# Sparse attention and a gated feed-forward block on one core: all transposes moved to TensorE

## The chip, the cores and the metric

The kernel runs on one core of one Trainium2 chip. Its engines are TensorE (PE; its weight loads are listed as PEld), VectorE (DVE), ScalarE (ACT), GpSimd (POOL) and SyncE (SP, which here only issues DMAs). The metric is the device time of one launch in microseconds (us), as the median of several runs. The profile is of one more execution, whose own time is given beside its span.

## The reference

Inputs are q, k and v of 4 batches, 8 heads, 768 positions and 64 dimensions, in float32, and the three matrices of a gated feed-forward block. Heads 0, 2 and 6 attend causally to everything; the other five see only the first 4 positions (the "sinks") and the last 64.

```python
def _attn_ref(q, k, v, is_retrieval, n_sink, window):
    scores = scale * np.matmul(q, k.transpose(0, 1, 3, 2))
    stream_keep = causal & (is_sink | in_win)
    mask = np.where(retr, full_mask, stream_mask)
    scores = np.where(mask[None, :, :, :], scores, -1000000000.0)
    a = np.exp(scores - np.max(scores, axis=-1, keepdims=True))
    a = a / (np.sum(a, axis=-1, keepdims=True) + 1e-09)
    return np.matmul(a, v)
# x: the heads side by side, 3072 x 512; d_ff = 1536
def _moe_ref(x, w_gate, w_val, w_out):
    g = x @ w_gate
    silu = g * (1.0 / (1.0 + np.exp(-g)))
    return silu * (x @ w_val) @ w_out
```

## The kernel before

**Tiles.** Positions are cut into 24 tiles of 128, six per batch. Two neighbouring tiles are a pair: 12 pairs in the order of the list `QP`, which takes batches 0 and 1 in turn and then 2 and 3. Four tiles make one of six groups `g` for the feed-forward part, whose moving operand is then 512 columns wide.

**Attention.** For a pair `n`, q, k and v (called `x` in the names of the loads) are loaded as float32 into one of 11 `raw` buffers (`load q5`), and cast to float16 (`cq5`, `ck5` into `hq`; `cx5.m.j` into `vt`). Queries and keys then have to be turned, so that the 64 dimensions (of two heads) lie on the partitions. There are two ways of doing that. For pairs 0 to 4 (`n < XPE`) PE turns eight 128x128 blocks with an identity matrix into one bank of PSUM (`trq`, `trk`, L473), and two copies on ACT or DVE take them to `qT` or `kT` (`evq5.m`, `evk5.m`, L206 and L208). For pairs 5 to 11 two transposing DMAs, issued on SP, do it from SBUF to SBUF (`dq5.m`, `dk5.m`, L463). The two ways leave positions in different orders, so the exponentials of the later pairs permute their output. Loads differ with them: pair 0 and pairs 5 to 11 are read in runs of 512 bytes by one DMA of 512 KB (L354), pairs 1 to 4 in runs of 2 KB by two DMAs of 256 KB (L349).

For a tile `t`, scores are made in up to four units (`sc5.0`, L567) in PSUM, ACT takes the exponential (`ex5.0`, L579), DVE or POOL multiplies with a 0/1 mask (`mask5.0`, L587; the first four tiles have the mask added by PE instead), PE multiplies with the values (`val5.1`, `val5.0`, L597) and DVE normalizes (`nm5`, L604 and L605) into `xb`. The columns of sink keys and values are copied to where later tiles find them (`sk`, `sv`).

**Outputs of attention.** `xb` has positions on the partitions; the feed-forward part needs features there. For tiles 0 to 7 (`t < XBAR`) PE turns four blocks (`xtr5`, L621) and ACT or DVE copies them into `xt` (`xe5`). For tiles 8 to 23 one transposing DMA on SP writes `xt` (`xdma8`, L615).

**Feed-forward.** For each group and each of 12 slices `j` of d_ff: four matmuls with gate weights (`gate2.3`, L759), a tanh on ACT (L765), a product on DVE (`stt1`, L769), four matmuls with value weights (`vals2.3`, L759 too), a product on DVE into `h_sb` (`stt2`, L775). The output product of groups 0 to 4 is done in seven products of half-size blocks in place of eight (`out2.p1` to `p7`, L839), with sums of `h_sb` blocks (`hs`, L826, POOL or DVE) ahead and sums out of PSUM (`oe`, L855, DVE) behind. Group 5 does it plainly (`out5`, L793). Results are stored by `st` on SP or ACT.

**What sets the order.** Every step is a task with dependencies, which are turned into semaphore waits. No scheduler runs: the string `ORDER` lists all tasks, in the order in which they are recorded, and each engine executes its own tasks in that order. `WAYS` says for each task which of the allowed engines does it (for example DVE or POOL for a mask), `SLOTS` which buffer of a ring, or which bank of PSUM, it takes. Numbers from 3700 up in `ORDER` are groups of warm-up matmuls (L321) for PE. Loads on SP stand in the same order, and a load waits there until its `raw` buffer is free, with all later DMAs of SP behind it.

Of the kernel before, what the change touches and what calls it, by code (L numbers as in the profile page):

```python
# [13 lines left out]


ORDER = (
    "0306071W091U1V1X000A08xy1c0D0C01050B1d1e040gy01f1gzJ1i1h2021282922232B1j1r1s021p1q1w0F2C2D2E2F1b"
    "2A2L2M2N2O2X2f2g0m1Y1a1Z1t1u1v1k0h252h1l1m2W2c242G2H2I2d2e2l2m2i2j0G271n1o1y1z3C262P2Q2R0z2t3031"
    "2J0y8e8o2n2K102U2o2p3I3J2V8t8j8m8u8v8k8l8n1x2k8f8g8p8q2x382y8h8i118r8s8w8x138y8z9893909495999A33"
    "340n9D9E0E2Z3K3D3L3M3N149B9C9F969G9H972a9192322b2Y2q2r2s2u3R3S3W3X0k1C9c9d9e9h9i9j3U3V3O2z353P36"  # L20
    "39370q1D9f9g9k9l3T3b3i3n3o3f3g0H3H3E3F2v2w0i169I9J9K9N9O9P0o179L9Q9R9M0l1F3Q3Y3Z3c3j3a0I3u40410j"
    "193k3h9m9n9o3l3m3A3B9S9T9U9r9s9t3d3e9X0J3v4344453G3p3q3r0r1G9u9p9v429Y9Z3s3t0x1H2S4647494A4H0p1A"
    "9V9WB74N4O4Q4R0K3z9q9zA10N4c3x4BB4B5B6B8Ak4K4L4V4b4C4D3yAT484M0w0sAQARASAU9a9b9y0t1E0W6K2TAlAmAV"
    "AWAX151M1O1N1PAYAZBEAfAgAhB9BABB4a0u181Q1R1SBCBDAp0v1BBFBGA0AaAbAnAoAc3wBHBIAdAe0L0M0PB20T12A41I"
    "1J1K0S4d4P0O4Z4h4g4Y4e4f5D5L5K0RAzB0B1AqArB31L0YALAM0ZAN4E4F4G4J4I6J1TAuAvAOAPAw9wA2A69xA3A7A55C"
    "5I5JAA4l4m4i4j4kACA8A9ABAD4n4v51524y53AiAj5f5lAEBMAGAFAK4S4z504T4W4UAxAy5g5nAsAtBL4q4r4o4p54BO0c"
    "AHAIAJ4s554t4u4x4wBJBKBQ56575T5U6MBNBP5W5c5XBb5j0X58595A5B707S7T6xBVBW6wBRBS5i5VBXBYBc6z5YBZBaBd"
    "5p5qBT5s605t5u4XBsBtBuCeCbCcCdCfCMCNCOCCBvBwCDCE0V6I5v0Q5F5G5H6v5k5o5M5N5O0UBiBjBk5rCPCQBlBm5E5Z"
    "5a5b5d5wCHCICJCWCXCY5m63696A666768Bh5h73CKCLC7C8C9710eCRCS5P5Q5R6465CACBCTBUC2C36y7Q6P74BnBo5x5y"
    "5z610a72CZCaBp5S625e6H6NBqBrC46B6C6F6D6GCFCGCiBeBfBgBxByBz7O7UC0C1C5C681CUCVCjCl6E6U6V6W6X6Y6R6S"  # L30
    "6T6eDmDjDkDlDnDoDpDqDrDs0b7P7X7WDtDuDv6Z6aCgChCn6b6c6d6fDUDVDWDXDY7576776g7C7D7E7F7G7L0dDwDxCkCm"
    "DSDFDGDHDPDQDRDT7b7c7d6QDADBDCDyDzE0DDDE7H80D5D6D7CsCt6O6n6o6h6i6j6kE1E27V7I7J7M7K7ND8D96l6m7879"
    "7A7BCoCpCrCuCv897Y7Z6p6q8786DKDLDMDZDaDb6L6r6s6t6uDcDdDeDfDgCwCx7e7f7R7j7m7n7o7p7q7rDNDOCyCzD0D4"
    "EhEiEjErEsEcEd88EkElEtCqD1D2D3EuEvEeDhDi7a7g7h7k7iFLFMFNFOFP7x8D8E8A8I8B8C8F8JFJFGFHFIFKFBFCFDDI"
    "DJE5E77s7t8GFEFFEp7u7v7y7w8HEXEYEZ0f838485EmEnEoEqEfEg8NEw8Y8ZE6E88T8U8VEzExEyF0EBE3E9E4EAECEDF6"
    "828K8L8M8OF1F2F3F9EFEG8Q8R8S8W8XEVEHEIEJF7F8FA7l8P7z8a8b8cEaEbESETEUEWEEEOELEM8dGiGMGTGUEKGCENER"
    "G7GVGWGjGkGJGKEPGREQFTFVGXGLGOGPGEGFGNGQG9F4GAGSGGGYGbGZF5GaGcGBGDFSGHFpFqFrFQFRG4G5GdGeFzFUFeFW"
    "FXGIG6G0G8FcFdGfFfFuFvFYFaFbGgGhG1G2G3FsFtFxGlGmFZFwFyFlFiFjFmFnFgFhFkFoGnGoGpGsGtGuGvGwGqGrGxGy"
    "GzH0H2H3H4H5H7H1H6H8H9"
)  # L40
WAYS = (
    "000010000000000000000000000000000000000000000000000000000000221202202202212200200111000111110010"
    "222200001100000000000000220022122022001011000000000000001100212002000011001001000001000001001000"
    "000201021120001000001001000000010010000010000000002221220000000000010000002000100100000020000221"
    "000000000100000002000010010000000000020200000010000000000000110000011000000100100000020001000000"
    "002202200220000000000000000012000100100000000201120000000000000000010002202202010000001001000001"
    "200000000000011002021000000000000000000200000000000000000000000000000000000000000000000000000000"
    "000000000000000000000000000000000000000000001000000000000000000000000000000000000000000000000000"
    "000000000000000000000000000000001000000010000000000000000000000000000000000000000000000000000000"
    "000000000000000000001110100011000000000001000000000000000000000000000000000000000000000000000000"  # L50
    "000000001111000001100000000000100000000000000000000000000000000000000000000000000000000000000111"
    "101100110000000000011000000000000000000000000000000000000000000000000000000000000000010000100000"
    "00000010"
)
SLOTS = (
    "0014237653916A152371476981504A39A2564807049A28352A9168410016041002241601230163620442561014104122"
    "636011642065221025144416322211256461406003404624344620616540610143626540604164236062324342142254"
    "041614064616325426212246140636104325614261306242452460436460636014122636230644521206164434062601"
    "020211341120003102001134000210400214105510131201001011040122021303213020111113411111040020200051"
    "014110101310002114301212131010022102320210013012111032112010000012000102211130011112010111054125"  # L60
    "001050101010110200030111402521014010311140310020120011321112001301101022015010340000101100015042"
    "1331142120102320202014112511225023512531113120100101201"
)
DIGITS = "0123456789ABCDEFGHIJKLMNOPQRSTUVWXYZabcdefghijklmnopqrstuvwxyz"

# [54 lines left out]
def kernel(  # L120
# [13 lines left out]
    nc = tc.nc  # L134
# [36 lines left out]
    P = Plan(RINGS)  # L171
# [38 lines left out]
    def recast(task, dst, src):  # L210
# [24 lines left out]
        out=ident, in_=ident, compare_op=ALU.not_equal, fill=1.0,  # L235
# [97 lines left out]

    XPE = 5
    XOLD = 1

    landed = {}
# [27 lines left out]
    for kd, n in ([(kd, n) for n in range(NP) for kd in "qkx"]  # L367
                  + [(kd, n) for kd in "gvo" for n in range(6)]):
        T_iss[kd, n] = P.add(f"load {kd}{n}", ["SP"], (lambda kd=kd, n=n: load(kd, n)),
                             takes=["raw"])  # L370
# [49 lines left out]
                                 (lambda i=i, x=x: wsum(i, x)),  # L420
                                 deps=[T_w["o", i][0], T_w["o", i + 3][0]] + before))

    XBAR = 8

    LEAD = 4

    hqs = {}
# [29 lines left out]
    def turned(n, kd):  # L457

        b, pi = QP[n]
        return qT[n % QB] if kd == "q" else kT[b % 2][:, 2 * pi:2 * pi + 2]  # L460

    def dmat(n, kd, m):
        nc.sync.dma_start_transpose(  # L463
            out=turned(n, kd)[:, m].rearrange("c k r (j n) -> c (k r j) n", j=2),
            in_=hqs[n, kd][m * 64:(m + 1) * 64].rearrange("p k a x -> p (k a x)"))

    trs = {}

# [100 lines left out]
    def exps(t, u, unit):  # L569
        e = es[t, u] = buf("e", [128, 8, 128], FH, "e")  # L570
        for p, s_, c, kt in unit[0]:
            h = PAIRS[p][s_]
            av_blocks.setdefault((t, h), []).append((e[:, c, :], value(t, h, kt)))
        at = slice(min(c for _, _, c, _ in unit[0]), unit[1])
        to, src = e[:, at], whole_sc.pop((t, u))[:, at]
        if t // 2 >= XPE:
            to = to.rearrange("p c (n j) -> p c n j", j=2)
            src = src.rearrange("p c (j n) -> p c n j", j=2)
        nc.scalar.activation(out=to, in_=src, func=AF.Exp, scale=scale)  # L579

    def mask(task, t, u, m):
# [27 lines left out]
    def xtranspose(t):  # L609
        xb = xbs.pop(t)  # L610
        g, n = GROUP[t]
        if g not in xts:
            xts[g] = buf("xt", [128, 4, 512], FH, "xt")
        if t >= XBAR:
            nc.sync.dma_start_transpose(  # L615
                out=xts[g][:, :, n * 128:(n + 1) * 128],
                in_=xb.rearrange("p a b d -> p (a b d)"))
            return
        tr = buf("gv", [128, 4, 128], FH, "xtr")
        for p in range(4):  # L620
            nc.tensor.transpose(tr[:, p, :], xb[:, p].rearrange("p a d -> p (a d)"), ident)  # L621
# [12 lines left out]
    def tasks_of_pair(n):  # L634
# [40 lines left out]
    def tasks_of_tile(t):  # L675
# [344 lines left out]
```

## Time and profile before

| | |
|---|---|
| median of 3 runs | 246.04 us (245.84 to 246.38) |
| profiled execution, its own time | 246.15 us |
| its span, first to last instruction | 244.4 us |
| granted TensorE clock | 1.00 of full speed |
| HBM read and written | 28.31 MB and 6.29 MB |
| gate and value matmuls, L759, 128x512 | 544, 216 ns from one to the next in a gapless stretch |
| PE transposes, L473 and L621 | 80 and 32, of 128x128 |
| transposing DMAs, L463 and L615 | 28 and 16, 1.2 us each to issue, 2.7 to 3.1 us to land (medians) |
| loads of q and k, L354 / L349 | 16 of 512 KB / 16 of 256 KB |

"Busy" is the time in which an engine had an instruction running; matmuls overlap, so the mean length of one (379 ns for 512 columns) is more than the time that it holds PE. The idle time of a group is what its engine waited just ahead of it, with the engine and line that released it. A released wait is put down to the last event seen.

### The profile page before, as it was taken

What the parts mean: (1) busy time and instruction counts of PE and PEld (TensorE: products, weight loads), DVE (VectorE), ACT (ScalarE), POOL (GpSimd) and SP (SyncE); (2) the same over time, 40 slices, a digit from 0 to 9 for tenths busy, and PEclk for the clock granted to TensorE, in tenths of its full rate; (3) what the DMA queues carried; (4) which work ended last, traced back from release to release, by engine and by line L of the source; (5) the groups of instructions that cost most, each with busy time, mean ns of one, the idle gap of its engine ahead of it and who ended that gap; (6) DMA issues with size and microseconds to landing.
All of it is one profiled execution on the core that took longest, in us unless ns stands there. A gap on an engine that the chain in (4) does not pass through costs nothing.

```text
span 244.4 us, 5604 instructions
## 1 busy us (share of the span) xinstructions
PE 234.5 (96%) x2189; PEld 143.6 (59%) x2189; DVE 186.7 (76%) x324; ACT 148.5 (61%) x235; POOL 129.0 (53%) x140
## 2 busy tenths in 40 slices
PE   7989999998999999799999999999999999999995
PEld 3667855553457678445555457656456764475743
DVE  0577887889999999887987977669769777776800
ACT  3899899887878669487637776563682302330011
POOL 7479999956497552375765446910094110375000
PEclk9999999999999999999999999999999999999999
DMA  6999999999766989999464451519100213100053
GB/s 187 355 348 353 323 352 366 313 362 305 206 131 78 287 165 289 191 268 192 89 130 130 97 120 38 90 36 234 38 4 0 46 21 115 59 0 1 7 203 136
DMA packets 66794, 40.73 MB, mean 167 GB/s; under 512 B 25168, under 2 KB 60240, under 8 KB 66768
## 3 DMA queue, kind: packets, MB, share of 16 engines
q1 hardware_dynamic: 65392, 37.76, 61.5%
q10 hardware_dynamic: 1376, 2.62, 2.9%
q8 instruction: 17, 0.28, 0.5%
q14 instruction: 9, 0.07, 0.1%
HBM read 28.31 MB, written 6.29 MB: 142 GB/s over the span
## 4 chain that ended last, share of the span: by engine, by line
PE 54%; DVE 19%; issue 8%; DMA 6%; POOL 5%; SPq 5%; ACT 2%; DVEq 0%; POOLq 0%
PE banks L759 34%; PE banks L839 10%; PE banks L793 4%; DMA raw<-in_moe_w_val_dram 4%; DVE h_sb L775 4%; PE banks L567 3%; DVE h_sb L826 3%; SPq L349 3%; DVE sil L769 3%; PE banks L597 2%; POOL hs_sb L826 2%; DVE out_sb L855 2%; DVE xb L605 2%; DMA xt<-xb 2%; DVE e L587 2%
## 5 line engine op out<-in xcount | busy, mean ns | idle before, releaser
L759 PE MATMUL banks<-xt,wg_sb 128*128 128x512 f16 (+1 forms) x304 | 70.3, 368 | 1.9 <-DMA xt<-xb 1.4
L759 PE MATMUL banks<-xt,wv_sb 128*128 128x512 f16 (+1 forms) x304 | 70.4, 368 | 0.8 <-DVE sil L769 0.7
L579 ACT ACTIVATE e<-banks 128x1024 f16<-128x1024 f32 (+2 forms) x68 | 58.7, 910 | 20.0 <-PE banks L567 11.7
L765 ACT ACTIVATE sig<-banks 128x512 f32<-128x512 f32 (+1 forms) x76 | 43.0, 577 | 43.5 <-PE banks L759 37.5
L769 DVE SCALAR_TENSOR_TENSOR sil<-sig,banks 128x512 f32<-128x512 f32 (+1 forms) x76 | 49.0, 656 | 14.8 <-ACT sig L765 12.6
L775 DVE SCALAR_TENSOR_TENSOR h_sb<-sil,banks 128x512 f16<-128x512 f32 (+1 forms) x76 | 48.7, 656 | 6.7 <-PE banks L759 4.4
L587 POOL TENSOR_TENSOR e<-e,m 128x640 f16<-128x640 f16 (+1 forms) x22 | 37.8, 1727 | 27.2 <-ACT e L579 24.3
L759 PEld LDWEIGHTS <-wg_sb 128*128 128x128 f16 x304 | 28.5, 98 | 30.7 <-issue 3.1
L759 PEld LDWEIGHTS <-wv_sb 128*128 128x128 f16 x304 | 28.2, 98 | 29.5 <-issue 1.2
L839 PEld LDWEIGHTS <-h_sb 128*128 128x128 f16 x360 | 34.8, 98 | 7.9 <-issue 0.7
L826 POOL TENSOR_TENSOR hs_sb<-h_sb 128x768 f16<-128x768 f16 x7 | 11.5, 1640 | 40.9 <-DVE h_sb L775 29.4
L855 DVE TENSOR_TENSOR out_sb<-banks,out_sb 128x512 f32<-128x512 f32 x35 | 23.6, 685 | 4.7 <-PE banks L839 4.4
L826 POOL TENSOR_TENSOR h_sb<-h_sb 128x768 f16<-128x768 f16 x11 | 18.0, 1639 | 8.2 <-PE banks L839 4.4
L839 PE MATMUL banks<-wo_sb,h_sb 128*128 128x256 f16 x180 | 21.9, 273 | 0.0
L839 PE MATMUL banks<-wt_sb,h_sb 128*128 128x256 f16 x180 | 21.5, 273 | 0.4 <-DVE out_sb L855 0.4
L567 PE MATMUL banks<-qT,kT 64*128 64x128 f16 x472 | 20.6, 218 | 1.1 <-DVE xb L605 1.0
L567 PEld LDWEIGHTS <-kT 64*128 64x128 f16 x472 | 14.6, 94 | 11.0 <-issue 10.2
L597 PEld LDWEIGHTS <-e 128*128 128x128 f16 x472 | 17.1, 97 | 4.3 <-ACT vt L206 0.9
L597 PE MATMUL banks<-vt,e 128*128 128x65 f16 x472 | 18.2, 193 | 1.0 <-POOL vt L208 0.7
L605 DVE TENSOR_TENSOR xb<-banks,rc 128x512 f16<-128x512 f32 x24 | 16.6, 691 | 0.8
L208 POOL CAST vt<-raw 64x512 f16<-64x512 f32 x22 | 14.4, 654 | 4.8 <-DMA raw<-in_v_dram 2.3
L206 ACT COPY out_sb<-banks 128x512 f32<-128x512 f32 (+1 forms) x7 | 4.0, 570 | 19.1 <-PE banks L793 16.0
(60 smaller groups left out, 216.3 us busy)
## 6 DMA issues: line engine op xcount, KB each, us to landing
raw<-in_v_dram SPq DMA_DIRECT2D x12, 512.0 KB, 7.0
raw<-in_q_dram SPq DMA_DIRECT2D x8, 512.0 KB, 4.8
raw<-in_k_dram SPq DMA_DIRECT2D x8, 512.0 KB, 5.1
raw<-in_moe_w_gate_dram SPq DMA_DIRECT2D x6, 512.0 KB, 8.9
raw<-in_moe_w_val_dram SPq DMA_DIRECT2D x6, 512.0 KB, 8.4
raw<-in_moe_w_out_dram SPq DMA_DIRECT2D x6, 512.0 KB, 7.9
out_dram<-out_sb SPq DMA_DIRECT2D x6, 512.0 KB, 4.7
raw<-in_q_dram SPq DMA_DIRECT2D x8, 256.0 KB, 6.4
```

The source lines that it names most:

```text
L567: nc.tensor.matmul(sc[:, c:c + n, :], weights, moving, start=first, stop=last)
L579: nc.scalar.activation(out=to, in_=src, func=AF.Exp, scale=scale)
L587: ENG[task().way].tensor_tensor(out=ev, in0=ev, in1=mm, op=ALU.mult)
L597: nc.tensor.matmul(avs[t][:, odd, n * 66:n * 66 + 65], ee, vv, start=(m == 0), stop=(m == len(bl) - 1))
L605: nc.vector.tensor_tensor(out=xb.rearrange("p n o d -> p o n d"), in0=av[:, :, :, 0:64], in1=rc.to_broadcast([128, 2, 4, 64]), op=ALU.mult)
L759: nc.tensor.matmul(ps, wsb[:, kk, j * 128:(j + 1) * 128], xt[:, kk, c[0]:c[1]], start=(kk == 0), stop=(kk == 3))
L765: nc.scalar.activation(out=sg[g, j, c], in_=gs[g, j, c], func=AF.Tanh, scale=0.5)
L769: nc.vector.scalar_tensor_tensor(out=sl[g, j, c], in0=sg.pop((g, j, c)), scalar=1.0, op0=ALU.add, in1=gs.pop((g, j, c)), op1=ALU.mult)
L775: nc.vector.scalar_tensor_tensor(out=hs[g, j][:, c[0]:c[1]], in0=sl.pop((g, j, c)), scalar=0.5, op0=ALU.mult, in1=vs.pop((g, j, c)), op1=A ...
L826: ENG[T_hs[g, x][part].way].tensor_tensor(out=to, in0=a, in1=b, op=op)
L839: nc.tensor.matmul(rooms[g, p][:, x], left[:, j, 128 * x:128 * x + 128], right[:, j], start=(j == 0), stop=(j == NK - 1))
L855: nc.vector.tensor_tensor(out=cell(*to), in0=rooms[g, p], in1=cell(*other), op=ALU.add)
```

## The change

- `XPE` goes from 5 to 12, so queries and keys of all pairs are turned by PE and copied out of PSUM, and pairs 1 to 11 are loaded in runs of 2 KB. `dmat` and its tasks go.
- `XBAR` goes: the attention outputs of all tiles are turned by PE (`xtr`) and copied by DVE or ACT (`xe`).
- The exponentials no longer permute positions for the later pairs.
- `ORDER`, `WAYS` and `SLOTS` are new throughout. By the lists of each engine's instructions, DVE and ACT between them get 28 more copies into `qT` and `kT` and 16 more into `xt`; nine masks go from DVE to POOL, and five sums `hs` too; four stores go from ACT to SP. The warm-up matmuls are 24 instead of 21.

```diff
-    XPE = 5
+    XPE = 12
     XOLD = 1
...
-    XBAR = 8
-
...
-    def dmat(n, kd, m):
-        nc.sync.dma_start_transpose(
-            out=turned(n, kd)[:, m].rearrange("c k r (j n) -> c (k r j) n", j=2),
-            in_=hqs[n, kd][m * 64:(m + 1) * 64].rearrange("p k a x -> p (k a x)"))
...
         to, src = e[:, at], whole_sc.pop((t, u))[:, at]
-        if t // 2 >= XPE:
-            to = to.rearrange("p c (n j) -> p c n j", j=2)
-            src = src.rearrange("p c (j n) -> p c n j", j=2)
         nc.scalar.activation(out=to, in_=src, func=AF.Exp, scale=scale)
...
-        if t >= XBAR:
-            nc.sync.dma_start_transpose(
-                out=xts[g][:, :, n * 128:(n + 1) * 128],
-                in_=xb.rearrange("p a b d -> p (a b d)"))
-            return
         tr = buf("gv", [128, 4, 128], FH, "xtr")
         for p in range(4):
             nc.tensor.transpose(tr[:, p, :], xb[:, p].rearrange("p a d -> p (a d)"), ident)
...
-            if n >= XPE:
-                T_ev[n, kd] = [P.lands(P.add(
-                    f"d{kd}{n}.{m}", ["SP"], (lambda n=n, kd=kd, m=m: dmat(n, kd, m)),
-                    deps=cs[kd] + old)) for m in range(2)]
-                P.uses(cs[kd][0], "hq", *T_ev[n, kd])
-                continue
             tr = P.add(f"tr{kd}{n}", ["PE"], (lambda n=n, kd=kd: transposes(n, kd)),
                        deps=cs[kd], takes=["gv"], after=[T_warm])
...
-        if t < XBAR:
-            xt = P.add(f"xtr{t}", ["PE"], (lambda t=t: xtranspose(t)),
-                       deps=norms, takes=["gv"] + takes, after=[lead])
-            T_xe[t] = P.add(f"xe{t}", ["DVE", "ACT"], (lambda t=t: xevac(t)), deps=[xt])
-            P.uses(xt, "gv", T_xe[t])
-            P.uses(norms[0], "xb", xt)
-        else:
-            xt = P.add(f"xdma{t}", ["SP"], (lambda t=t: xtranspose(t)), deps=norms,
-                       takes=takes, after=[lead])
-            T_xe[t] = P.lands(xt)
-            P.uses(norms[0], "xb", T_xe[t])
+        xt = P.add(f"xtr{t}", ["PE"], (lambda t=t: xtranspose(t)),
+                   deps=norms, takes=["gv"] + takes, after=[lead])
+        T_xe[t] = P.add(f"xe{t}", ["DVE", "ACT"], (lambda t=t: xevac(t)), deps=[xt])
+        P.uses(xt, "gv", T_xe[t])
+        P.uses(norms[0], "xb", xt)
```

More of the change, by code (lines that the diff above doesn't have):

```diff
@@ L16 @@
 ORDER = (
[L17 to L36, printed above, removed]
@@ L37 @@
-    "G7GVGWGjGkGJGKEPGREQFTFVGXGLGOGPGEGFGNGQG9F4GAGSGGGYGbGZF5GaGcGBGDFSGHFpFqFrFQFRG4G5GdGeFzFUFeFW"
-    "FXGIG6G0G8FcFdGfFfFuFvFYFaFbGgGhG1G2G3FsFtFxGlGmFZFwFyFlFiFjFmFnFgFhFkFoGnGoGpGsGtGuGvGwGqGrGxGy"
-    "GzH0H2H3H4H5H7H1H6H8H9"
+    "000402061U1V071W03xx1c1d1e0920211Xy21f0C01050A22yG28292A231g1h1i1j1r1s1p1q1w081Z1b1axh2B2CzG2E2D"
+    "2F2N2O2L2M2W2c2d2e0B2426252G2H2I0D2X2f1Y1k1l1m1t1u1v2g2i2h2j2l2m1n2J1o1y1z2K272P2Q2R0g0y98999A1x"
+    "2t30312x382y0F3C3I3J3K0h139c9S9T9d9U0m109B9C0n140G2o2p33349e0z9I2S2U2V9D9G9h9a9E9F9H9i9j2n9V9W0E"
@@ new lines @@
+    "2Y2a2Z9X9Y9Z9f9g9b9J9K3D3L2b2k2q2r2s2u3M3N3O3P3U3V329k9l0i169r9m9s9t2z9n9o3R3S353637399N9O119L9M"
+    "9P9Q9R0H3F3H3E3b3l3m3i3j0l1FALAGAMANAH3W3X3f0o179u9v9pAI9q3T3G0q1D3Q3Y3Z3a3g3c0k1CA6ABA7A83kA9AA"
+    "ACAD2T0j3n3o0t19A19wA23h3p3q2v3r3A3B2w3d3e0r1GAJAKA3AOAP3s3t0J3v439x9y0I3u4041420p1AA4A50K3y3x3z"
+    "Ax0U15AEAFATAV4446454748494H4A4BB40wAuAvAwAy9zA00P5J0M4b0u18ASB5B6BEBFBGBdBeBf0s12B7B84L4M4NB9BA"
+    "BBBYBZBgBhBaBC1E1M3w0V4O4P4W4CBbBc4DAUBDAzB0B14j4k4l0RBiBjBk0x1H1Q1R1T1S4E4F4GBHBIBlBm0vB2B31B1K"
@@ new lines @@
+    "1I1J1LAY1N1P0L4a4g4h4i5R0N4d4f4e4cAQAXARAZAW4p4qBTBUBVBOBPBQ4m4z4R4S5S5TApAqAr0bBWBX1OAe0O5I0Y7E"
+    "4n4oBJBKBL0S0e4Q5O5P5Q4I0W6X6YAcAdAfAiAj4r56574J4KAaAbAgAhAkAo4T4U4V4X53AsAt5p5v5w54554u4v4s4t5f"
+    "BMBN4w5g4x4y505c5l5dBRBSBpBrBnBo5B5C595A58AlAm4Y4Z515D5E5F5xBv0T5s5t520a5q5y5z60BqBsBuByC5Bt6465"
+    "0cAnBw616C625G5HC10Z7H66D5D6D7CCCDCECoD8D90Q5L5K5NClCmCnCp7mCRCSCTCgChCi5h6J6KBzC07M7N7O5rCjCk0X"
+    "7D5M5e5i5j5k5mC36VC2C4C6C7CB7I6W6L5U5V5W6G6H6ID0D1D2CvCwCFCGCxCe5X5Y5ZCMCNCyCzCO7lD3D467685u7k6M"
@@ new lines @@
+    "6N6e6f6gCUCV6b6c6d63696A6B6DCPCQCqCrCs5a5n5b5o7q7r7s6O6P6Q6SCbCcCdCf7J7K6E6FCWCXCYBxC8C9CA7L6R6h"
+    "6i6j6k6l6uCtCu6T6UCKCZCaDDDFCHCICJENEOEPCLDCDE6mEDEEEFDtDuDv7t7u7v0f8T6n6o6p6qEIEJ0d8QDADGDBDH7o"
+    "7X7Y7Z7a7g7b7cDwDxEKELEMEGEH6r6s6v6tDIDLDJ8U74757172737P7Q7RDeDfDgDyDzE0EQERDZDaDb7z807G76DhDiES"
+    "ETEUE1E2EVEW6aDMDN7F7d777e7f7S7T7U8RDm6y6z707w7xDcDd6w6x7i7V7W7j7pE3E4E5DODPDj6Z78797AE881DkDlDn"
+    "8W8X8Y7B7CDoDpDqEB7nFBFCFD878H8I8B8CE9DQDR7yE6E7EA8E8MEC8283FLFMFNFEFFDrDs7h848588868ZFOFPFn8D8F"
@@ new lines @@
+    "8G8a8b8c8k8l8f8g8h8d8e8VFGFHFIFaFbFcF6F7F8FiFVFWDKF9FAFXDSEZDUEaDTEbFkFlFJFKFmDYFfFgDVDWFoFhFj8J"
+    "8K8N8LEXEYEdFpFqFrFsFtFQFRFS8p91928w8xFdFe8i8j8tFTEcElEe8S8m8n8o8q8uEfEi8vF1F2EjF3En8z90EwExEhFU"
+    "Es8y9394DXEkEmEgEo898r8A958s8OF49697EpEqErEtEz8PGxHCHDGnFxFzEyH2GyF5GbGzGqEvGoEuF0GpGrGiGjH0H5Gk"
+    "GvH3H1H4H6GsGtGuGwFYFZGlGYGZGaGcGJGKGLFuFvFwFyG0G2G4GdGeGfGmH7H8H9GRGgGhGOGPGTHEGUG1G6G7G5GFHAG3"
+    "GCHBGVGWGXGAGQGSHFHGGMGNG8G9GDGGGHHHGBGEGIHIHJHMHNHKHLHOHRHPHQHSHTHWHXHYHbHUHVHZHaHcHd"
@@ L40 @@
 )
 WAYS = (
[L42 to L51, printed above, removed]
@@ L52 @@
-    "101100110000000000011000000000000000000000000000000000000000000000000000000000000000010000100000"
-    "00000010"
+    "000010000000000000000000000000000000000000000000000000000000222202022222202002220010101010101212"
+    "020000000000000000000000110001212222011011000000100000001000220011011000001001000001001001001000"
+    "000001220111011000001001000000010000010010000000002201120000000000010000000010010010000011000200"
+    "200010010010010000000210100100000000000020102000001100000001001001000010002221101000000100100000"
@@ new lines @@
+    "020000100100000120120000201100000000100000002200001001000000000220112000000001000000010010001101"
+    "201110001001000001000001101001001000001201102020000000001000000000010010000010000000000000000000"
+    "000000000000000000000000000000000000000000000000000000000000000000000000100000000100000000000000"
+    "000000000000000000000000000000000000000000000000000000000000001001000100000000000000000000000000"
+    "000000000000000000000000000000000000000000000000001111110011000000000000000000000000000000000000"
@@ L54 @@
+    "000000000000000000000000000000000000000111110000100000000000100000000000000000000000000000000000"
+    "000000000000000000000000000111110100110000000000000000000000000000000000000000000000000000000000"
+    "00000000000000000000000010000000000010"
 )
 SLOTS = (
-    "0014237653916A152371476981504A39A2564807049A28352A9168410016041002241601230163620442561014104122"
-    "636011642065221025144416322211256461406003404624344620616540610143626540604164236062324342142254"
-    "041614064616325426212246140636104325614261306242452460436460636014122636230644521206164434062601"
@@ L59 @@
[L59 to L62, printed above, removed]
+    "0015246374927435A772A445A6315997824058A38A501609221819001016041002241222230063601254461440016340"
+    "656011214224222121043652064614232261606014354644521622063602461221046162644040343654462621302145"
@@ new lines @@
+    "600160216141211426361623606445601310362216320614025604224614041421402642562542516163424201406465"
+    "604133263222541412634461606200005010410210124411031120024500140040110012330130002110011155022233"
+    "031050200011002221015001401011100100401441250120510120130251113012411115121401501220005100430000"
+    "013110000200100345500000202121500000211114301100125115412010041125124052131203005501111211023311"
+    "1112131134100412210200023310531201144125302011050100012411241100410131043120200002102"
```

## The prediction

> **What bounds the kernel now.** I read the page's busy shares first, then the busy time by stage, then the chain that ended last, and last the groups by shape.
>
> ```profile
> PE 234.5 (96%) x2189; PEld 143.6 (59%) x2189; DVE 186.7 (76%) x324; ACT 148.5 (61%) x235; POOL 129.0 (53%) x140
> ```
>
> Busy time in five stages from the first value matmuls on (columns: stretch, its length, then PE, PEld, DVE, ACT, POOL busy, granted clock, DMA share, GB/s):
>
> ```profile
> 22.65:61.00 38.35, 37.60 (x393) 22.63 (x393) 32.66 (x65) 34.23 (x58) 32.59 (x34) 1.00 1.11 337
> 61.00:100.00 39.00, 38.16 (x402) 26.86 (x399) 37.96 (x64) 28.84 (x42) 21.32 (x19) 1.00 0.89 186
> 100.00:140.00 40.00, 38.25 (x332) 20.49 (x333) 32.89 (x58) 26.65 (x43) 24.72 (x21) 1.00 0.78 161
> 140.00:200.00 60.00, 59.12 (x574) 37.25 (x573) 46.16 (x77) 31.37 (x50) 23.11 (x21) 1.00 0.32 66
> 200.00:244.40 44.40, 41.38 (x247) 23.40 (x244) 25.05 (x39) 9.29 (x16) 11.40 (x7) 1.00 0.19 72
> ```
>
> PE idles 0.75, 0.84, 1.75 and 0.88 us in the four stages up to 200 us, 4.22 us in 177. Nothing else is so full, except DVE between 61 and 100 us (37.96 of 39.00). DMA is full only until about 61 us. Pieces of the chain that ended last (start, length, what):
>
> ```profile
> 28.34 0.45 PE banks L473 x8
> ...
> 45.64 0.22 PE banks L621 x4
> ...
> 95.85 0.50 SPq L615
> 96.40 4.70 DMA xt<-xb
> 101.24 5.34 PE banks L759 x24
> ...
> 200.24 13.81 PE banks L759 x64
> ...
> 230.99 10.40 PE banks L793 x60
> ```
>
> Three things are in it. From 200 us to the end PE runs without a gap (64 matmuls of 512 columns in 13.81 us are 0.216 us each), so anything that delays PE before 200 us delays the end. The one place where a transposing DMA holds PE is at 101.24. And it prices the operations that the change multiplies: eight L473 transposes hold PE for 0.45 us, 0.056 us each, and four L621 transposes for 0.22 us, 0.055 each. The 0.22 us "mean of one" in the groups is latency, which overlaps.
>
> [...]
>
> **PE, added.** Pairs 5 to 11 get PE transposes for q and k: 7 x 2 x 8 = 112 at 0.056 us = 6.3 us. Tiles 8 to 23 get four each: 64 at 0.055 = 3.5 us. Together +9.8 us of PE time, in the new order all between about 60 and 200 us, where PE has 4.22 us free in all. Nothing PE does is taken away there: scores, values, gates and products are the same in number and shape. Lower end: if all 4.22 us of idle were filled, +5.6. Upper end: were each group to hold PE for its whole latency (0.62 us for eight L473, 0.40 for four L621, from the timeline of PE), 14 x 0.62 + 16 x 0.40 = 15.1. I take 9.8, since the groups in the chain, which stand between other matmuls, hold PE for just 0.45 and 0.22.
>
> [...]
>
> **PE, removed.** The wait at 101.24 for the first transposing DMA of tile 8 (idle 1.4 us, "DMA xt<-xb" in the groups): -1.4. It is the only PE wait put down to a DMA; q and k transposes by DMA have none. Ends: 0, if the PSUM copy that replaces it is as late, and -1.5.
>
> **What is late next.** Each group now needs a copy out of PSUM before its reader can run, on ACT or DVE, in their order. I walked the new order of PE and looked for readers that stand within 2.2 us of PE work behind their transposes. After 60 us there are six: trk7 before sc14.1 (1.3 us: out1.p5), trk11 before sc22.0 (1.7), trq5 before sc10.1 (1.8), xtr11 before gate2.11 (1.3), xtr17 before gate4.3 (1.7), xtr23 before gate5.8 (2.2). A pair of ACT copies takes 1.06 us (2 x 0.59, overlapped), so each is covered unless one or more other instructions stand ahead of the copy: for k of pair 7 it is xe10, 0.59. Bounds: 0 to 6 x 0.59 = 3.5 us. I take one copy's length, 0.6, since most have cover and PE's queue behind the waiting matmul is then stopped (here all of group 2's gates). The other waits of PE in the old order (4.22 - 1.4 = 2.8 us up to 200) belong to that order; the new one has its own, by the same kinds of edges, and I carry them over at equal size, 0 net, with -2.8 as the end if they go.
>
> **The other engines.** ACT gets 14 kT, 5 qT and 9 xt copies (0.588, 0.590, 0.586 us): +16.5, and gives up casts and sink copies, net +7.7. DVE gets 9 qT and 7 xt copies (0.683, 0.419): +9.1, plus value casts, but nine masks leave it, net +4.1. POOL takes those masks (five at 2.122, four at 1.397 us: 16.2) and five more sums at 1.64, net about +26. I price all of this at 0: ACT is 52 to 74% busy from 61 to 200 us, POOL 39 to 62%. DVE is the one to fear: up to the last value matmuls of tile 11 (93.9 us now) its work grows by 1.8 us, but PE's grows by 2.2 by then. If that cover went, the price would be those 1.8 us. POOL's masks are slow (2.1 us against 0.784 on DVE) and in front of the value matmuls; a mask that is late costs at most the 1.3 us difference, which is inside the 3.5.
>
> **Loads and queues.** Fourteen loads of 512 KB in 512-byte runs become 28 of 256 KB in 2 KB runs, an extra 14 issues on SP at 0.60 us (L349), 8.4 us. From the same queue go 44 transposing issues at about 1.2 us, 53 us. All of it lies after the first 30 us, where SP is not what PE waits for: price 0. Stores move from ACT to SP, and four waits there end later, 0. The early loads are the same in bytes and shape; v0 goes behind g1 and k2 back two places. By the same landing times gate0.2 would take v0's place, so the head moves by no more than one load, within 0.6 us either way. Exponentials lose a permuted write: the rows of old and new kinds of tile are both 1.02 us, 0. Three more warm-up matmuls stand in the head, where PE waits for loads, 0.
>
> **Sum.** 246.15 (the profiled execution: 244.4 of span and 1.8 around it) + 9.8 - 1.4 + 0.6 = 255.15. The median of the runs is 0.11 lower than that execution, so 255.0.
>
> **Rivals.** *The new order closes PE's gaps.* All the idle of the four stages goes: 246.04 + 9.8 - 4.2 + 0 = 251.6, and 250 if the head gains a load or two (0.6 each, twice) as well. For it: nearly all of that idle is edges of the order. Against: the new order has more tight edges than the old. Chance 0.15.
>
> *The evacuations bind.* The tight places each wait and the long masks on POOL delay value matmuls, as DVE does now at 91.0: 255.0 + 2.9 + 1.3 = 259.2, between 257.5 and 262. For it: DVE at 97% until 100 us and 28 more copies out of PSUM on ACT. Against: ACT's shares above. Chance 0.17.
>
> *The head shrinks, and it is faster.* Of the first 22.65 us PE spends 7.0 on 21 warm-up matmuls and 2.65 idle; were the loads so ordered that the gates start 9.65 us sooner, the sum would be 255.0 - 9.65 = 245.3. It decides from a gain of 9 us on. Against: POOL waits until 18.80 for the first gate weights to land, and these are the ninth load in both orders. Chance 0.05.
>
> *It does not do what it says:* excluded, the list of PE's instructions has the transposes of all 12 pairs and 24 tiles, and SP's has no transposing DMA left.
>
> **How the numbers follow.** Forecast 255.0, chance 0.63, its own range 252.5 to 257.5 (2.5 down is most of the 2.8 of idle, 2.5 up most of 2.9 more waits). The range runs from 250.0, the second case with its head, to 259.5, the middle of the third: left out are the faster case (0.05), a little of the second (0.03) and the upper half of the third (0.09). About 0.2% (0.5 us) is what a measurement of this kernel can tell from no change. Faster 0.05, within it 0.01, slower 0.94.
>
> **What would show it.** Right: PE busy near 244 at about 96%, the last stage from the group-5 gates on as gapless as now and shifted by 9 us, L466 at 0.45 us for eight and L606 at 0.22 for four, no PE idle put down to a DMA after 60 us, six or fewer new waits of PE for kT, qT or xt copies of under 0.6 us each. Wrong: PE idle before the last stage well under 2 us (second case) or above 8 with ACT or DVE copies as releasers (third); transposes at more than 0.07 us apiece; a first gate before 15 us.

## The result and the profile after

| | before | after |
|---|---|---|
| median | 246.06 us (245.84 to 246.38) | 258.83 us (258.66 to 259.27) |
| ratio, with its 95% interval | | 1.052 (1.0502 to 1.0539) |
| profiled execution, its own time | 246.15 us | 258.92 us |
| its span | 244.4 us | 256.9 us |

The change makes the kernel 12.8 us slower. The forecast was 9.0 us slower: inside the range, but 3.8 us short, and outside the likeliest case's own range of 252.5 to 257.5. The granted clock is 1.00 in both.

The first line of the page after, busy time of each engine:

```profile
PE 246.9 (96%) x2368; PEld 153.8 (60%) x2368; DVE 195.2 (76%) x337; ACT 154.8 (60%) x245; POOL 154.7 (60%) x161
```

PE's busy time has grown by 12.4 us, the span by 12.5. Its idle time is the same, 10.0 us against 9.9. So the added time is, in sum, time in which PE runs, and yet the transposes account for only 10.4 of it, as is worked out below.

The same by stretches, cut at PE's first gate matmul, at its 40th step of the feed-forward part, at two points inside, and at the last group's gates (length, then PE, PEld, DVE, ACT, POOL busy, clock, DMA share, GB/s):

```profile
21.41:63.40 41.99, 39.60 (x409) 24.12 (x409) 38.58 (x75) 31.43 (x52) 34.75 (x33) 1.00 1.06 346
63.40:103.00 39.60, 38.00 (x422) 26.38 (x421) 35.30 (x60) 28.29 (x45) 28.30 (x25) 1.00 0.50 150
103.00:145.00 42.00, 42.00 (x405) 25.62 (x404) 35.82 (x61) 30.89 (x51) 25.60 (x22) 1.00 0.28 88
145.00:211.83 66.83, 66.60 (x671) 42.45 (x670) 48.71 (x81) 38.35 (x59) 39.78 (x36) 1.00 0.05 17
211.83:256.90 45.07, 42.01 (x249) 23.63 (x246) 26.60 (x41) 9.20 (x16) 11.45 (x7) 1.00 0.19 71
```

PE's idle time in the four stretches up to the last is 2.39, 1.60, 0.00 and 0.23 us, 4.22 in all. Before had 4.30 from its first gate matmul to 200 us: 0.83 up to its 40th step (20.53 to 61.32) and 3.47 behind it. So the sum is the same, but the idle time has moved: the middle of the kernel is now packed, and the early stretch loses 2.4 us instead of 0.8. DMA's share in the third and fourth stretch is 28% and 5%; it buys nothing, since PE is what is full.

Pieces of the chain that ended last, after (start, length, what):

```profile
101.74 0.45 PE banks L466 x8
...
104.05 0.33 PE banks L606 x4
...
161.74 0.67 PE banks L606 x12
...
211.83 13.81 PE banks L732 x64
...
243.45 10.40 PE banks L766 x60
```

In these pieces eight transposes of q or k hold PE for 0.45 us, four of x for 0.33 and twelve for 0.67. The wait of the old kernel at 101.24 for a transposing DMA is gone; PE works through that place. The last group's gates run as gapless as before, 11.6 us later (211.83 against 200.24).

**Where the 12.5 us lie.** I numbered PE's gate, value and output-product steps in the order in which they start, and compared the start of the n-th in both traces. What a matmul holds of PE is counted from its start to the start of the next one, less PE's idle time between them.

| part | before to after, us | made of |
|---|---|---|
| up to the first gate matmul (20.53 to 21.41) | +0.88 | the head |
| steps 0 to 40 (to 61.32 and 63.35) | +1.16 | PE's idle time +1.56, its work -0.4 (nine score matmuls fewer) |
| steps 40 to 170 | +10.42 | 14 groups of q/k transposes 6.78, 16 groups of x 3.59, everything else +0.05 |
| after that | 0.0 | |

The +0.05 is not a stretch in which nothing else changed. PE's idle time there fell by 1.64 us (3.47 to 1.83). Against that stand 17 score matmuls, which before had done earlier (8 of them in the head, 9 up to step 40), with 1.05 us, and 0.6 us by which the same number of value, gate and product matmuls hold PE longer.

### The profile page after: what moved, and what is told of

Read it like the earlier page. It is cut to its first block, busy times and chain, and to the rows that moved or that the text cites. A ratio compares the mean times of both kernels' runs of the same rounds, so it can differ in the third digit from the quotient of the medians.

```text
span 256.9 us, 5969 instructions
## 1 busy us (share of the span) xinstructions
PE 246.9 (96%) x2368; PEld 153.8 (60%) x2368; DVE 195.2 (76%) x337; ACT 154.8 (60%) x245; POOL 154.7 (60%) x161
## 4 chain that ended last, share of the span: by engine, by line
PE 65%; POOL 11%; DVE 9%; DMA 6%; SPq 5%; issue 3%; POOLq 0%; DVEq 0%
PE banks L732 33%; PE banks L812 16%; POOL e L577 7%; PE banks L560 4%; PE banks L766 4%; SPq L349 4%; DMA raw<-in_moe_w_val_dram 3%; PE banks L587 3%; DMA raw<-in_moe_w_out_dram 2%; DVE h_sb L748 2%; DVE wt_sb L412 2%; PE banks L466 2%; PE banks L606 1%; POOL wg_sb L208 1%; POOL wv_sb L208 1%
## 5 line engine op out<-in xcount | busy, mean ns | idle before, releaser
L732 PE MATMUL banks<-xt,wg_sb 128*128 128x512 f16 (+1 forms) x304 | 71.2, 368 | 3.1 <-DVE sil L742 1.7
L732 PE MATMUL banks<-xt,wv_sb 128*128 128x512 f16 (+1 forms) x304 | 70.8, 368 | 0.0
L577 POOL TENSOR_TENSOR e<-e,m 128x640 f16<-128x640 f16 (+1 forms) x31 | 54.8, 1783 | 19.8 <-ACT e L569 19.3
L732 PEld LDWEIGHTS <-wg_sb 128*128 128x128 f16 x304 | 28.0, 97 | 31.7 <-issue 4.7
L732 PEld LDWEIGHTS <-wv_sb 128*128 128x128 f16 x304 | 28.4, 98 | 27.8 <-issue 0.2
L799 POOL TENSOR_TENSOR hs_sb<-h_sb 128x768 f16<-128x768 f16 x8 | 13.3, 1668 | 27.9 <-DVE h_sb L748 21.0
L799 POOL TENSOR_TENSOR h_sb<-h_sb 128x768 f16<-128x768 f16 x13 | 21.4, 1642 | 6.2 <-PE banks L812 5.0
L560 PE MATMUL banks<-qT,kT 64*128 64x128 f16 x472 | 21.6, 218 | 0.5 <-DVE xb L595 0.3
L560 PEld LDWEIGHTS <-kT 64*128 64x128 f16 x472 | 14.6, 94 | 11.6 <-issue 10.1
L208 POOL CAST hq<-raw 128x1024 f16<-128x1024 f32 (+1 forms) x16 | 16.1, 1014 | 4.0 <-DMA raw<-in_k_dram 2.9
L466 PE MATMUL banks<-ident,hq 128*128 128x128 f16 x192 | 14.6, 219 | 1.7 <-DVE h_sb L748 1.0
```

The source lines that it names most:

```text
L208: ENG[task.way].tensor_copy(out=dst, in_=src)
L560: nc.tensor.matmul(sc[:, c:c + n, :], weights, moving, start=first, stop=last)
L577: ENG[task().way].tensor_tensor(out=ev, in0=ev, in1=mm, op=ALU.mult)
L732: nc.tensor.matmul(ps, wsb[:, kk, j * 128:(j + 1) * 128], xt[:, kk, c[0]:c[1]], start=(kk == 0), stop=(kk == 3))
L799: ENG[T_hs[g, x][part].way].tensor_tensor(out=to, in0=a, in1=b, op=op)
```

## The experiments

Where a kernel leaves work out, its expectation says which.

### Fewer transposes on PE

```diff
-        for j in range(8):
+        for j in range(8 if n < 5 else 1):
             nc.tensor.transpose(tr[:, j], hqs[n, kd][:, j // 4, j % 4], ident)
+        if n >= 5:
+            trs[n, kd] = tr[:, 0:1].to_broadcast([128, 8, 128])
...
-        for p in range(4):
+        for p in range(4 if t < 8 else 1):
...
-        trs[t] = tr
+        trs[t] = tr if t < 8 else tr[:, 0:1].to_broadcast([128, 4, 128])
```

> The changed kernel with one PE transpose left in each added group (of 8 for q and k of pairs 5 to 11, of 4 for tiles 8 to 23); the copy out of PSUM keeps its full size and reads that one block several times, so the results of those pairs are not attention. Left out: 14 x 7 + 16 x 3 = 146 transposes of 0.056 us, 8.2 us. Theory (PE is the bound, the transposes' own PE time is the cost): 258.8 - 8.2 = 250.6, within 0.7. Rival (the readers wait for the copies out of PSUM, on ACT and DVE): the copies and their waits are all still there, so less than half of it comes back, 255 or more.

Measured: 257.84 us (257.52 to 258.3), ratio to before 1.0485 (1.0463 to 1.0507). Of the 146 transposes left out (8.2 us at 0.056 each) only 1.0 us came back. "PE's time is the cost, so without it the time falls" does not hold in this order. The chain of waits, its shares by engine, says what took PE's place; first after, then this kernel:

```profile
PE 65%; POOL 11%; DVE 9%; DMA 6%; SPq 5%; issue 3%; POOLq 0%; DVEq 0%
```

```profile
PE 52%; DVE 29%; issue 5%; POOL 4%; SPq 4%; ACT 3%; DMA 2%; DVEq 0%; POOLq 0%; ACTq 0%
```

DVE's part of the chain goes from 9 to 29%. PE's idle time rises from 10.0 to 14.2 us (255.4 of span less 241.2 busy). Between steps 40 and 170 the transposes hold PE for 7.3 us less, but PE's waits there grow by 4.3 us, and the other matmuls hold it for 1.4 us longer. The copies take as long as in after (those of q 592 ns on ACT and 685 on DVE).

### A quarter of each copy

The same program as after, but the copies of q and k of pairs 6 to 11 out of PSUM move a quarter of their columns.

```diff
+        fs = slice(0, 4 if n < 6 else 1)
...
-            copy(T_ev[n, kd][m], dst.rearrange("c (f n j) -> c f n j", f=4, j=8),
+            copy(T_ev[n, kd][m], dst.rearrange("c (f n j) -> c f n j", f=4, j=8)[:, fs],
```

> The changed kernel with the PSUM copies of q and k of pairs 6 to 11 (24 copies) cut to a quarter of their columns; the rest of qT and kT keeps older data there. PE's work is the same. It takes some 0.3 us from each copy, about 7 us off ACT and DVE together. Theory (PE bound): 258.2 to 258.9, no more than the few waits at those copies. Rival (copies bind): each group's readers come 0.6 us sooner, 254 to 257.

Measured: 258.96 us (258.75 to 259.33), ratio 1.0526 (1.0503 to 1.055). Step by step its profile lies 0.50 us behind after's from the first gate on and stays there, 0.49 at the end: nothing is won anywhere, though a copy now takes 0.27 to 0.28 us instead of 0.59 to 0.69. The length of these 24 copies is not on the path.

### The two added warm-up groups taken out

`ORDER` without its last two groups of warm-up matmuls, three in all.

> The changed kernel with 21 warm-up matmuls instead of 24 (the last three, two groups after the first scores, left out), as many as the kernel before has. Theory: the first gate matmul comes 0.88 us later than before, and 0.64 of that is the time the fillers hold PE, so the head shortens by about 0.6: 258.2. Rival (in the head PE waits for loads, and the fillers only fill that): 258.8, the time unchanged within 0.2.

Measured: 259.21 us (258.77 to 260.02), ratio 1.0545 (1.052 to 1.057). The first gate starts at 21.29 instead of 21.41, since PE idles for 0.55 us more in the head. The warm-up matmuls are not what makes the head longer.

### Four early casts of values from DVE to ACT

`WAYS` of `cx2.1.0`, `cx2.1.1`, `cx3.1.0` and `cx3.1.1`, and their places in `ORDER`.

> The changed kernel with four casts of values of pairs 2 and 3 (0.68 us each on DVE) moved from DVE to ACT, next to the casts of the same pairs that ACT has already. In the first 40 gate and value steps the changed kernel loses 1.16 us, and PE waits there for DVE's products. Theory (DVE is the bound of that stretch, 92% busy there against 85% before): 0.8 to 1.4 us back, 257.4 to 258.0. Rival (POOL's masks and the loads set that stretch, DVE only passes it on): within 0.3 of 258.8, or slower since ACT's exponentials come later.

Measured: 258.52 us (258.45 to 259.63), ratio 1.0527 (1.0502 to 1.0551). In its profile 0.65 us is won by step 40 (0.21 of it in the head), and a wait of 0.8 us appears at 100 us, where value matmuls wait for a mask on DVE; the end is 0.33 us later than after's. The profile of the kernel without the three warm-up matmuls has the same wait (0.95), after's does not. The profiled execution took 259.42 us, 0.9 more than the median, so the median may well be without this wait. The medians differ by 0.3 us, which lies within after's own runs (258.66 to 259.27).

### PE and DVE relieved, then POOL too, then the two without PE

Three kernels: the first two edits together, and the masks of tiles 8 to 23 left out where DVE has them; then all of those masks; then the copies and all masks, with every transpose kept.

```diff
     def mask(task, t, u, m):
+        if t >= 8 and task().way == "DVE":   # the second kernel and the third: if t >= 8:
+            return
```

> The changed kernel with PE relieved (one transpose in each added group, 8.2 us less of PE) and DVE relieved as well (the q and k copies of pairs 6 to 11 a quarter wide, and DVE's seven masks of tiles 8 and up left out, some 10 us less of DVE; the attention of those tiles is not the reference's). PE alone gave back 1.0 us. Theory (PE and DVE are both full between 60 and 145 us, so that neither alone gives anything back): 252 to 255. Rival (POOL's masks and sums, in front of value matmuls and products, are the second bound): 256.5 or more.

> As the run with PE and DVE relieved, and POOL's masks of tiles 8 and up left out too (24 masks, some 43 us of POOL). Theory (PE and DVE are the two bounds): within 1 us of that run, since POOL was not a bound. Rival (POOL is the second bound): 249 to 252, several us below it.

> The changed kernel with all its PE transposes, but DVE and POOL relieved (q and k copies of pairs 6 to 11 a quarter wide, all masks of tiles 8 and up left out). Theory (PE is as full as the others: it idles 1.8 us between 63 and 212 us): 256.8 to 258.3, so each relief alone gives little and only both together give the 8 us. Rival (the engines behind PE are the bound and PE merely follows them): 251 to 254.

| left out | time, us | ratio to before |
|---|---|---|
| nothing (after) | 258.83 | 1.052 (1.0502 to 1.0539) |
| transposes | 257.84 | 1.0485 (1.0463 to 1.0507) |
| copies in part, all masks | 257.86 | 1.0462 (1.0447 to 1.0478) |
| transposes, copies in part, DVE's masks | 255.41 | 1.0372 (1.0353 to 1.039) |
| transposes, copies in part, all masks | 254.75 | 1.0343 (1.0326 to 1.036) |

PE relieved alone gives 1.0 us, the other two alone 1.0, all together 4.1 (by the ratios, which set each against before in the same session, 0.9, 1.4 and 4.4). Step by step, in the profiles, these gains lie in different places:

| left out | steps 0 to 40, us | steps 40 to 170, us |
|---|---|---|
| nothing (after) | 41.95 | 162.13 |
| transposes | 41.95 | 160.61 |
| copies in part, all masks | 40.57 | 162.06 |
| transposes, copies in part, DVE's masks | 40.57 | 160.90, at a mean granted clock of 0.993 over this profile |
| transposes, copies in part, all masks | 40.78 | 159.45 |

In the early stage it is DVE's masks that count, and there is just one of them up to step 40. Behind step 40 nothing comes back from DVE and POOL as long as PE has all its transposes: there PE sets the time. If PE is relieved as well, 2.7 us come back, where the transposes alone gave 1.5. And with all of it gone the kernel is still some 8 us above before, 5.2 of them PE's busy time (239.7 against 234.5) and 3.2 its idle time. In the last one PE waits for other reasons, its waits by releaser (us in total, times, longest):

```profile
PE banks L737 <- DVE xt L208: 2.0, 2, 1.5
PE banks L737 <- DVE sil L747: 1.6, 3, 0.7
```

The gates (here L737) stand behind the copy of an x transpose that has itself just been made. In this order, fixed beforehand, time taken out ahead of such a round trip made the wait longer: the gates wait 0.5 us for `xt` copies on DVE in after, 1.7 without the transposes and 2.0 here.

### The old kernel with 9.7 us of PE added

```diff
+        if wsb is wg_sb and (1 <= g <= 3 or g == 4 and j < 9):
+            nc.tensor.matmul(ps, wsb[:, 0, j * 128:(j + 1) * 128], xt[:, 0, c[0]:c[1]],
+                             start=True, stop=True)
```

> The kernel before with 45 more matmuls of 512 columns on PE and nothing else: the first of the four matmuls of a gate step is done twice for groups 1 to 3 and nine steps of group 4. 45 x 0.216 = 9.7 us of PE, as much as the added transposes, in the same stretch (60 to 200 us), without their copies and in the old order. Theory (PE's idle there is 3.5 us, the rest of the added time shows): 246.1 + 6.5 to 9.7 = 252.5 to 255.8. Rival (added PE time is hidden by the waits for DVE and POOL, and it is the new order that costs): 247 to 250.

Measured: 253.66 us (252.55 to 254.96) beside 246.46 for before, ratio 1.0297 (1.0259 to 1.0334). 45 matmuls of 0.216 us are 9.7; 7.2 show (6.1 to 8.5 in the single runs). So PE does bound the old kernel: three quarters of this PE time is paid, with no new transposes, copies or order.

### The parts alone, in the old order

Three kernels made from before. The new transposes stand in `ORDER` a few steps behind the norm or cast that feeds them, their copies some steps further, in PSUM banks chosen to fit the old plan; the other work stays in its old order and on its old engines. First the two tiles whose DMAs end PE's wait at 101.24:

```diff
-    XBAR = 8
+    XBAR = (*range(8), 9, 11)
...
-        if t >= XBAR:
+        if t not in XBAR:
...
-        if t < XBAR:
+        if t in XBAR:
```

> The kernel before in its old order, with tiles 9 and 11 alone (the two whose transposing DMAs end PE's wait of 1.37 us at 101.24) turned by PE and copied by ACT. Theory, the forecast's second term: the wait is a true price on the path, so the time falls by about 1.4 less 8 transposes of 0.055 us: 246.2 - 1.4 + 0.44 = 245.2 (244.8 to 245.6). Rival: DVE's or POOL's chain stands as late there, the wait only changes its name, and the time is 246.2 to 247.0.

Measured: 245.76 us (245.48 to 246.47) beside 246.41, ratio 0.9972 (0.995 to 0.9994). Step by step it is 1.03 us ahead by step 72, which is the wait of 1.37 less 8 transposes (0.44), gives back 0.37 between steps 96 and 104, and ends 0.66 ahead. The wait was a true price. This kernel is faster than after, and ahead of before by 0.3%, which the interval only just tells from no change. Its chain at that place, where before's had the DMA:

```profile
96.97 0.11 PE banks L621 x2
97.09 2.62 PE banks L839 x24
99.71 0.55 PE banks L567 x16
100.26 5.29 PE banks L759 x24
```

Then all x of tiles 8 to 23 (`XBAR = 24`, copies on ACT), and that with q and k of pairs 5 to 11 (`XPE = 12`, copies on the engines that the change gives them):

> The kernel before in its old order, with x of tiles 8 to 23 by PE (64 transposes, copies on ACT) and the queries and keys still by DMA. Theory, the PE time shows in full and the wait at 101.24 goes: 246.2 + 64 x 0.055 - 1.4 = 248.3 (247.7 to 249.0). Rival, each transposing group brings a wait for its copy as well: 249.7 or more. A third, that the old order hides a quarter of added PE time as it did with the 45 repeated matmuls (7.2 of 9.7 us): 246.2 + 2.6 - 1.4 = 247.4.

> Everything that the change moves to TensorE (x of tiles 8 to 23, queries and keys of pairs 5 to 11, and 2 KB runs in the loads of pairs 5 to 11), but in the old order with the new instructions put in where the transposing DMAs were issued. Theory: the transposes cost their PE time, of which the old order hides at most a quarter, and the new order is what costs the rest (the longer early stage, 2.0 us, and DVE and POOL as late as PE): 246.2 + 10.4 x 0.74 to 1.0 - 1.4 to 0 = 252.5 to 256.6, likeliest 254.5. Rival, the order is not at fault and everything above the PE time comes with the operations themselves: 258 or more.

Measured: 252.02 us (252.0 to 252.36), ratio 1.0228 (1.0186 to 1.0269), and 265.38 us (265.14 to 265.73), ratio 1.0765 (1.0721 to 1.0809). The x kernel costs more than its PE time, but not by waits for copies, as its rival had it: PE waits 3.6 us just ahead of its x transposes. And my theory, that the new order is what costs the rest, falls: with the same operations the old order, with the transposes put in by hand like this, is 6.6 us slower than the new one (6.0 by the ratios). Another way of putting them in wasn't tried. In spans, the x kernel has 3.9 us more PE busy and 1.9 more idle than before; the one with both has 11.8 more busy and 7.2 more idle. The groups of transposes, q/k and then x, in the one with both (busy, mean ns, idle of PE just before them):

```profile
L473 PE MATMUL banks<-ident,hq 128*128 128x128 f16 x192 | 14.5, 219 | 4.0 <-DVE sil L769 1.8 <-DVE out_sb L855 1.3 <-POOL hq L208 0.5
...
L621 PE MATMUL banks<-ident,xb 128*128 128x128 f16 x96 | 8.5, 220 | 3.7 <-DVE xb L605 1.6 <-ACT e L579 1.5 <-DVE h_sb L775 0.6
```

and in after:

```profile
L466 PE MATMUL banks<-ident,hq 128*128 128x128 f16 x192 | 14.6, 219 | 1.7 <-DVE h_sb L748 1.0 <-POOL hq L208 0.7
...
L606 PE MATMUL banks<-ident,xb 128*128 128x128 f16 x96 | 7.7, 219 | 0.0
```

7.7 us of waiting just ahead of transposes there, 1.7 here. A transpose reads `hq` or `xb`, and some 2.1 of the 7.7 us are waits for these. It reads neither `sil` nor `out_sb` nor `e`: those releasers are the last readers of the PSUM bank that it is to write (all of PSUM is one set of eight banks in this kernel). The timeline of PE shows two of them in the kernel with both, the wait in brackets:

```profile
81.91 0.61 PE L473 MATMUL banks<-ident,hq 128*128 128x128 f16 x8 [1.27 <-DVE out_sb L855]
...
98.61 0.38 PE L621 MATMUL banks<-ident,xb 128*128 128x128 f16 x4 [1.53 <-ACT e L579]
```

The transposing DMAs go from SBUF to SBUF here and take no bank; before has one PE wait for a DMA, of 1.4 us. The new `ORDER` and `SLOTS` avoid most of the waits for a bank.

### The old order up to the 24th step, the new one behind it

`ORDER`, `WAYS` and `SLOTS` only.

> The changed kernel with its first 238 steps of ORDER (up to the 24th gate, value or output step of PE, 43.35 us in its profile) put back into the order of the kernel before (which is there at 42.02), the rest as changed, and four PSUM banks given anew at the join. Theory, the longer early stage is a true price: 1.3 us by the join, up to 2.2 with the steps that the old order has done ahead there: 258.8 - 1.3 to 2.2 = 256.6 to 257.5. Rival, what is won is lost again in the tight order behind it, as when four value casts went from DVE to ACT: 258.2 to 258.9.

Measured: 260.72 us (259.59 to 261.02), ratio 1.0563 (1.0539 to 1.0587). Neither theory: at step 24 it is just 0.47 us ahead of after, and between steps 24 and 32 it loses 4.0, in waits at the join (1.44 us for a value cast, 0.91 for a copy of x, 1.17 for an exponential) and in a clock that fell to 0.50, of which more below. As a test of the early stage it is void. It shows two other things. The first gate is back at 20.55, so the longer head is a matter of the order. And 2.11 us late at step 40, it is 2.35 late at the end, 190 us on: this delay of PE is carried to the end.

## Why the prediction was right, and where it was short

**The bound, right.** PE sets the time: the kernel before pays 7.2 of 9.7 us of added PE work, and the last group's gates and products after are as gapless as foretold.

**The transposes, right in size.** Forecast 9.8 (6.3 for q/k, 3.5 for x), measured 10.4 in the table of steps (6.78 and 3.59). A group of x holds PE for the 0.22 us of the forecast, a group of q or k for 0.48 instead of 0.45.

**The wait for the DMA and the new waits, right in kind and short in size.** Forecast -1.4 and +0.6, so -0.8. The wait did go, and the two-tile kernel shows that it was worth about what was said. (The forecast reads it as the wait for the first transposing DMA, of tile 8. It is for the last of the group's four, issued at 96.40 and landed at 101.10.) New waits came, 1.0 us of transposes for `h_sb` and 0.6 of gates for a `qT` copy among them; the first is a wait for a bank, which the forecast, with its prices for copies alone, did not have. Together PE's idle time behind step 40 fell by 1.64. That gain does not show in the time, since the forecast put at nothing what stands against it: 17 score matmuls that the new order does later (1.05 us) and 0.6 us of other matmuls that hold PE longer.

**The head and the early stage, wrong by 2.0, the largest miss.** Both were priced at 0, the head within 0.6 either way. They belong to the new order and not to the transposes: in the six profiles with the old order up to there, the one with all the transposes among them, the first gate starts at 20.47 to 20.55, in the eight with the new one at 21.10 to 21.93.

The head took 0.88. Its last long wait is for POOL in both kernels, and ends at nearly the same time; what differs is how much PE has to do from there to the first gate. First before, then after:

```profile
17.75 0.42 PE L597 MATMUL banks<-vt,e 128*128 128x65 f16 x8 [0.71 <-POOL vt L208]
...
20.53 1.05 PE L759 MATMUL banks<-xt,wg_sb 128*128 128x256 f16 x8
```

```profile
17.70 0.62 PE L466 MATMUL banks<-ident,hq 128*128 128x128 f16 x8 [0.70 <-POOL hq L208]
...
21.41 0.60 PE L732 MATMUL banks<-xt,wg_sb 128*128 128x256 f16 x4
```

Less the short waits in between (0.19 and 0.26 us) that is 2.59 us of work before and 3.45 after. The forecast looked at the loads and the warm-up matmuls. The first value weights now land at 23.07 instead of 21.55, after the first gate has begun, so they are not what delays it.

The next 40 steps took 1.16. There DVE is busy 38.58 of 41.99 us, where before had 34.76 of 40.77, and PE waits for it:

```profile
56.63 1.81 DVE e L577
...
58.73 0.70 DVE sil L742
...
59.47 1.89 PE banks L732 x8
```

The wait ahead of 59.47 is 1.22 us long, and what stands in front of it on DVE is a mask, which takes 1.89 us beside a mask and a cast on POOL, where one alone takes 0.67 to 0.69. The three kernels without this mask have steps 0 to 40 in 40.57 to 40.78 us, no more than before's 40.79. The chain of the one that keeps POOL's masks has no wait at that place:

```profile
54.77 5.33 PE banks L737 x24
```

The kernels without the transposes alone (41.95) or with the short copies alone (41.96) don't differ from after there, so it is the mask that costs the early stage its time. How much of that is its slowness and how much the mask itself, no run shows. DVE was "the one to fear" in the forecast, with a price of 1.8 if its cover went, and that is what happened, but the forecast looked at DVE's total up to 93.9 us and took no account of a mask that becomes slower beside POOL. The seven value casts on DVE instead of three play a smaller part: with four of them on ACT the stage takes 0.44 us less, and other waits stand in place of this one.

**Sum.** 9.0 + 2.0 (early) + 0.6 (transposes) + 0.8 (behind step 40, other PE work of 1.7 less 0.8 of waits beyond the forecast) = 12.4, of 12.5 in the spans. The remaining 0.3 of the 12.8 lies outside the span (2.0 us around it instead of 1.75). That the time lies inside the range is due to the width of the range: the transposes and the bound were right, and the miss is nearly all in terms that were put at nothing.

**The rivals.** The time lies in the interval of "the evacuations bind" (257.5 to 262). Its mechanism is not what happened: PE's idle time before the last stage is 4.22 us, not above 8, and copies of a quarter of the size change nothing; only its long masks on POOL had a part, by way of DVE. "The new order closes PE's gaps" was right for 63 to 212 us, where 1.83 us of idle is left of 3.5, and the early stage gave that back. The head grew.

**What fell after the prediction.** I took for granted that a cost made of PE time would come back if PE had less to do. In this order it does not (1.0 of 8.2 us): waits for DVE and for the round trips of the order take its place. And I came to blame the order for what went beyond the PE time; the old order with the same work, as I put it in, is worse. What remains: of the 12.8 us, 10.4 are time in which PE transposes, in a stretch where PE has next to no idle time and where relief of DVE and POOL gives nothing back; 2.0 are what the new order pays early. Whether an order with fewer transposes could use the time that they leave is not shown.

## What to carry to other kernels

Moving transposes from a DMA queue that is not waited for to the engine that sets the time added their time to that engine here, 10.4 us against one wait of 1.4; where only those were moved whose DMA is waited for, nothing was lost (two tiles, -0.3%). A PE transpose here also takes a PSUM bank and a place in PE's queue, so where it stands counts beside what it costs: the same operations took 6.6 us more in a plan not made for them. In an order that is fixed beforehand, leaving work out is a poor measure of what it costs: PE relieved alone gave 1.0 us back, DVE and POOL alone 1.0, all of them 4.1, and only a count by stages told which gain came from where.

## What the runs showed of the hardware

**Masks on DVE are slower beside POOL.** The same form of mask on DVE takes 784 ns on average before and 1207 ns after, where POOL has more masks of its own. First before, then after:

```profile
L587 DVE TENSOR_TENSOR e<-e,m 128x1024 f16<-128x1024 f16 x10 | 7.8, 784 | 2.4 <-ACT e L579 2.4
```

```profile
L577 DVE TENSOR_TENSOR e<-e,m 128x1024 f16<-128x1024 f16 x5 | 6.0, 1207 | 0.6 <-ACT e L569 0.5
```

Of the fifteen, the ten with POOL idle, or busy for no more than 0.11 us beside them, take 0.67 to 0.69 us; the five with POOL at work nearly all the time take 1.00, 1.16, 1.36, 1.62 and 1.89. DVE's busy time grew by 8.5 us where the rows of before made it 4.1; the seven masks left on DVE took 8.05 us, and 4.9 by the rows of before, which is 3.2 of the difference. So three of the five that DVE keeps after run beside POOL's work, and take 1.16, 1.62 and 1.89 us. What makes them slower there is not shown.

**The clock fell after short gaps.** In the kernel with the join, PE was idle in two gaps of 1.44 and 0.91 us within four, and the granted clock went from 1.00 to 0.50. Stretches of 1 us (length, PE busy, clock, DMA share, GB/s):

```profile
46.00:47.00 1.00, 0.54 (x3) 1.00 0.82 239
47.00:48.00 1.00, 0.02 (x1) 1.00 0.18 54
48.00:49.00 1.00, 1.00 (x31) 1.00 0.00 0
49.00:50.00 1.00, 0.45 (x9) 1.00 0.61 129
50.00:51.00 1.00, 0.65 (x2) 0.65 1.07 322
51.00:52.00 1.00, 1.00 (x3) 0.50 0.89 301
```

The chain has `50.35 3.53 PE banks L732 x8`: 0.44 us for a matmul that takes 0.216, some 1.8 us on top of the 2.4 of the gaps. The clock was at 1.00 again from 54 us on. Two other profiles have a mean clock of 0.993 in place of 1.00. In that of the old kernel with more PE work the page has it at 0.7 in one of the 40 slices, from 101.3 to 107.6 us, and at 0.9 or more in all others; PE has a single wait of 2.0 us there, its longest. The other is that of the kernel with PE and DVE relieved. It does not always happen: after single gaps of 1.36 us (before, at 101.24) and 1.53 (the old order with both, at 98.61) the clock stays at 1.00. In the kernel with the join PE had been busy for 2.01 of the four microseconds (46 to 50 us) before the clock fell; how much idle time it takes, these runs do not settle.
